# Loads of k and stores of the output with an outermost dimension of 32 or more rows, in a thresholded-attention and MoE kernel

## The chip, the cores and the metric

The kernel runs on one core of one Trainium2 chip. The metric is device microseconds of one execution. Each time below is the median of a kernel's runs, and every experiment ran beside the kernel before on the same chip (983.7, 983.4, 982.4, 985.3 and 989.2 us in the five sets), so sets can be compared through that.

Five engines work side by side: PE (matrix products; PEld in the views is its weight loads), DVE, ACT and POOL (elementwise work), and SP, which here only issues DMA transfers. Sixteen DMA engines carry out the transfers.

## The reference

```python
# q, k, v: (8 batches, 8 heads, 576 rows, 64), float32; w_in: 512 x 2048; w_out: 2048 x 512
scores = q @ k.T / 8
scores = where(scores >= max(scores) - 0.02, scores, -1e9)
attn = softmax(scores)
x = (attn @ v)                      # heads side by side: (4608, 512)
h = x @ w_in
out = maximum(0.01 * h, h) @ w_out  # (4608, 512), float32
```

## The kernel before

The work is cut into 160 steps, 20 to a batch of the inputs: five row chunks `c` times four head pairs `p`. A step computes scores on PE, finds the row maximum on DVE, takes the exponentials on ACT (`E` for one head; for the other a scaled copy `P`, whose exponential goes into `w` a step later), masks on DVE, divides by the sum on POOL (`w`), turns `w` around with a transposing DMA (`wt`), and multiplies by v on PE five steps later (`LAG`). MoE products are spread between the steps. Meanwhile each batch prepares k and q of the next one: load, cast to two float16 halves on ACT and POOL (`ks`, `qs`, two buffers each), transpose by DMA (`kst`, `qst`).

The parts that the change and the argument touch:

```python
    def load_qk(b, hb):
        ...
        src_q = q[b, ds(4 * hb, 4), :, :].rearrange("(g h) (p t) d -> h p g (t d)", h=2, t=9)
        src_k = k[b, ds(4 * hb, 4), :, :].rearrange("(g h) (x p t) d -> x h p g (t d)", h=2, x=2, t=9)
        for g in range(2):
            for x in range(2):
                nc.sync.dma_start(out=km[ds(64 * x, 64), g, :], in_=src_k[x, :, :, g, :])
            if b == 0:
                nc.sync.dma_start(out=qm[:, g, :], in_=src_q[:, :, g, :])
        ...
    def rows_of(b, c):
        if c == 4:
            return out[ds(b * S, 2 * S), :].rearrange("(b p t) d -> t b p d", t=9, b=2)[8]
        return out[ds(b * S, S), :].rearrange("(p t) d -> t p d", t=9)[ds(2 * c, 2)]
    # ... cut: the steps; a finished group of 128 rows is stored with
    nc.sync.dma_start(out=G.stores[m], in_=osb)
    # ... cut: the main loop, at the end of each step
        if evac:
            evac()
        for t in tick.get(s, []):   # loads, casts and transposes that prepare the next batch
            t()
```

A k load takes 32 rows of each of two heads, which don't join into one run of rows, so its outermost dimension is the two heads. A store takes two rows (2c and 2c+1) of each of 64 groups of nine, written with those two outermost: 2 x 64 x 512.

The order in which instructions stand on each engine is not the order of this text: a scheduler sets it when the program is built, and the engines then keep to it.

Of the kernel before, what the change touches and what calls it, by code (L numbers as in the profile page):

```python
# [12 lines left out]
AF = mybir.ActivationFunctionType  # L13
# [3 lines left out]
def kernel(  # L17
# [16 lines left out]
    nc = tc.nc  # L34
    B, H, S, D = q.shape
# [39 lines left out]
    def load_qk(b, hb):  # L75


        qm = sb.tile([128, 2, 576], FP32, tag="qm", bufs=2, name="qm")
        km = sb.tile([128, 2, 576], FP32, tag="km", bufs=2, name="km")
        src_q = q[b, ds(4 * hb, 4), :, :].rearrange("(g h) (p t) d -> h p g (t d)", h=2, t=9)  # L80
        src_k = k[b, ds(4 * hb, 4), :, :].rearrange("(g h) (x p t) d -> x h p g (t d)", h=2, x=2, t=9)
        for g in range(2):
            for x in range(2):
                nc.sync.dma_start(out=km[ds(64 * x, 64), g, :], in_=src_k[x, :, :, g, :])
            if b == 0:
                nc.sync.dma_start(out=qm[:, g, :], in_=src_q[:, :, g, :])
        if b > 0:
            nc.sync.dma_start(out=qm[:, :, :], in_=src_q)
        qms[b, hb], kms[b, hb] = qm, km

    def load_v(b):
# [106 lines left out]
    def h_unit(G, u):  # L198
        n = G.n
        per = 512 // n  # L200

        def mms():
            if u == 0:
                G.g = sb.tile([128, NJ, 256], FP16, tag="gT", bufs=2, name="gT")[:, :, 0:n]
            hp = ps.tile([128, per, n], FP32, tag="h", bufs=2, name="hp")
            for jj in range(per):
                j = u * per + jj
                for g in range(4):
                    nc.tensor.matmul(  # L209
                        out=hp[:, jj, :], lhsT=w_in16[:, g, ts(j, 128)], rhs=G.x[:, g, :],  # L210
                        start=(g == 0), stop=(g == 3), skip_group_check=True,
                    )

            def act():
                nc.scalar.activation(out=G.g[:, ds(u * per, per), :], in_=hp, func=AF.Relu, bias=0.0, scale=0.99)  # L215
                if (u + 1) * per == NJ:
                    for m in range(n // 128):
                        for c in range(4):
                            oq.append(lambda m=m, c=c: o_unit(G, m, c))
            return act  # L220
        return mms
# [47 lines left out]
    def rows_of(b, c):  # L269

        if c == 4:
            return out[ds(b * S, 2 * S), :].rearrange("(b p t) d -> t b p d", t=9, b=2)[8]
        return out[ds(b * S, S), :].rearrange("(p t) d -> t p d", t=9)[ds(2 * c, 2)]


    steps = []
# [9 lines left out]
    def group_of(b, c):  # L286

        if c == 4:
            key = ("t", b // 4)
            if key not in groups:  # L290
                t = b // 4
                groups[key] = Group(256, [rows_of(4 * t + 2 * m, 4) for m in range(2)])
            return groups[key], 64 * (b % 4), b % 4 == 3
        if b == B - 1 and c >= 2:
            if (b, c) not in groups:
                groups[b, c] = Group(128, [rows_of(b, c)])
            return groups[b, c], 0, True
        key = (b, c // 2, 0)
        if key not in groups:
            groups[key] = Group(256, [rows_of(b, 2 * (c // 2) + cc) for cc in range(2)])  # L300
        return groups[key], 128 * (c % 2), c % 2 == 1
# [41 lines left out]
    def pv(s):  # L343
        b, c, p = steps[s]
        wt = st[s]["wt"]
        vt = vts[b]
        n = 128 if c < 4 else 64
        if p == 0:
            pvt[0] = ps.tile([128, NP, n], FP32, tag="pv", bufs=1, name="pv")
        pvp = pvt[0]  # L350
        for j in range(5):
            for h in range(2):
                rhs = wt[:, 5 * h + j, :] if c < 4 else wt[:, j, ds(64 * h, 64)]
                nc.tensor.matmul(  # L354
                    out=pvp[ds(64 * h, 64), p, :], lhsT=vt[:, 2 * p + h, j, :], rhs=rhs,
                    start=(j == 0), stop=(j == 4), skip_group_check=True,
                    tile_position=(0, 64 * h),
                )
        if p == NP - 1:
            G, col, done = group_of(b, c)  # L360

            def evac():
                nc.scalar.activation(out=G.x[:, :, ds(col, n)], in_=pvp, func=AF.Copy, bias=0.0, scale=1.0)
                if done:
                    for u in range(NJ * G.n // 512):
                        hq.append(h_unit(G, u))
            return evac
        return None
# [30 lines left out]


    load_qk(0, 0)
    load_qk(0, 1)
    prep_q = deque()
    for p in range(NP):
# [9 lines left out]
    for g in range(4):  # L414
        nc.gpsimd.dma_start(
            out=w_out16[:, ds(4 * g, 4), :],
            in_=moe_w_out[ds(512 * g, 512), :].rearrange("(j p) d -> p j d", p=128))

    tick = {}
    for b in range(1, B):  # L420
        s0 = 20 * (b - 1)
        tick.setdefault(max(0, s0 - 4), []).append(lambda b=b: load_qk(b, 0))
        tick.setdefault(s0 + 12, []).append(lambda b=b: load_v(b))
        tick.setdefault(s0 + 4, []).append(lambda b=b: load_qk(b, 1))
        for p in range(NP):
            for i, t in enumerate(prep_tasks(b, p)):
                tick.setdefault(s0 + 1 + 4 * p + (i * 4) // 7, []).append(t)
# [7 lines left out]
    for s in range(NS + LAG + 1):  # L435
# [15 lines left out]
        if live:  # L451
            d = st[s]
# [19 lines left out]
        if live:  # L472
            nc.vector.scalar_tensor_tensor(  # L473
                out=d["W"][:, 0, 0:576], in0=s32, scalar=tb[:, 0:1], in1=E,
# [22 lines left out]
    while hq or oq:  # L497
        for q_ in (hq, oq):
            if q_:
                f = q_.popleft()()  # L500
# [37 lines left out]
```

## Time and profile before

| | before |
|---|---|
| time | 983.67 us (981.94 to 985.41) |
| PE, DVE, ACT, POOL busy | 61%, 54%, 46%, 45% |
| mean granted clock of PE | 0.857 |
| DMA engines, hardware queue | 87.6% of their time in packets |
| bytes moved | 115.8 MB, 118 GB/s |

Lines of the page of the kernel before. PEclk, DMA and GB/s have one value for each of 40 slices of the span, in tenths of full for the first two; q1 is the hardware DMA queue with packets, MB and share of 16 engines' span.

```profile
span 981.9 us, 14544 instructions
...
PE 600.4 (61%) x4880; PEld 373.7 (38%) x4880; DVE 528.8 (54%) x1580; ACT 453.2 (46%) x894; POOL 439.7 (45%) x572
...
PEclk9999977787858876878679997878799899989999
DMA  3999989999979699999999999998897998849720
...
q1 hardware_dynamic: 324768, 105.94, 87.6%
```

No compute engine is near full, but the DMA row is at 9 almost everywhere. In this count a DMA engine is busy while a packet is under way, also while that packet waits (18 packets that stand still for over 4 us are shown below).

The list of waits of the kernel before: who waited for what, us in total, how often, the longest.

```profile
ACT qs L155 <- DMA qst<-qs: 143.5, 25, 15.0
PE pv L354 <- DMA wt<-w: 117.1, 30, 11.2
...
PE sc L326 <- DMA qst<-qs: 107.6, 5, 55.7
```

PE and ACT wait for transposes. One place shows why. This is the timeline of the kernel before between 417 and 431 us; columns are start, duration, engine, line, operation, and in brackets the idle time just before and what ended it. A span on SPq is the time that SP took to issue.

```profile
417.08 0.58 SPq L241 DMA_DIRECT2D out_dram<-osb  x1
...
418.77 11.96 SPq L397 DMA_TRANSPOSE wt<-w  x4
...
421.33 0.47 PE L354 MATMUL pv<-wt,v 128*64 128x128 f16 x10 [0.52 <-ACT xT L363]
...
429.05 0.74 PE L354 MATMUL pv<-wt,v 128*64 128x128 f16 x10 [7.24 <-DMA wt<-w]
```

A store is issued at 417.08. The transposes behind it take long to issue, and PE stands idle for 7.24 us because a transpose hasn't landed. The packets that started in each microsecond of that stretch, counted from the trace's packet records (2,048 B are the store's, 256 B the transposes'; the k and q loads' left out):

```
us      store packets   transpose packets
420          11               278
421          24               192
422          26                 0
423          24                 0
424          26                 0
425          17                36
426           0              1015
```

While the store drains, at about 25 packets a microsecond of 84 ns each, so with two packets in flight, no transpose packet starts for three microseconds; when it ends, over a thousand start in one. The transposes are not merely queued: 18 of their packets, started by 421.9 us, stay in flight until 426.05 to 426.10 us, just after the store's last packet ended at 425.87. Over the whole span, two-engine copies (0.5 to 5 packets of a k load or store in flight, averaged over 0.1 us) are in flight for 427 us, and in 370 us of that fewer than 10 transposes' packets start in 0.1 us, against 73 otherwise when they flow. Wider copies (more than 5 packets in flight) run for 40 us.

### The profile page before, as it was taken

Reading aid. Unit: us, or ns where it says so; the run is one execution under the profiler, and the core shown is the slowest. Engines: PE = TensorE matmul, PEld = TensorE weight load, DVE = VectorE, ACT = ScalarE, POOL = GpSimd, SP = SyncE. Lnnn points to the kernel's source line nnn. Section 1 sums busy time; section 2 is a strip of 40 time slices with the busy share of each in tenths; the row PEclk is TensorE's granted clock in tenths of the full one; section 3 lists DMA queues with packets and bytes.
Section 4 is the critical chain, followed back from the end, with each engine's and each line's share of the span. In section 5 each row is a group of like instructions: output and inputs, shape, how many; then the busy total and the mean of one; then the engine's idle time right before and its main releaser. Section 6 shows DMA issues by size and latency. Waiting matters only on the chain. (4 is left out here: it accounts for less than half of the span.)

```text
span 981.9 us, 14544 instructions
## 1 busy us (share of the span) xinstructions
PE 600.4 (61%) x4880; PEld 373.7 (38%) x4880; DVE 528.8 (54%) x1580; ACT 453.2 (46%) x894; POOL 439.7 (45%) x572
## 2 busy tenths in 40 slices
PE   0010457555547534764549874775599669799995
PEld 0000133333324322542335542443366445565662
DVE  0040276564756614645438763654578568777800
ACT  2020255463644523544436563544567556665820
POOL 4250276273645533335535563624665654443500
PEclk9999977787858876878679997878799899989999
DMA  3999989999979699999999999998897998849720
GB/s 83 101 140 83 134 160 176 120 139 127 146 91 143 99 116 97 129 137 125 126 102 135 120 139 98 120 132 116 131 166 98 143 142 107 109 85 107 104 59 33
DMA packets 348651, 115.78 MB, mean 118 GB/s; under 512 B 333216, under 2 KB 335264, under 8 KB 348576
## 3 DMA queue, kind: packets, MB, share of 16 engines
q1 hardware_dynamic: 324768, 105.94, 87.6%
q0 software_dynamic: 23808, 8.92, 10.9%
q8 instruction: 38, 0.62, 0.3%
q14 instruction: 37, 0.30, 0.2%
HBM read 36.70 MB, written 9.44 MB: 47 GB/s over the span
## 5 line engine op out<-in xcount | busy, mean ns | idle before, releaser
L392 POOL TENSOR_SCALAR w<-w,rc 128x576 f16<-128x576 f16 x288 | 248.3, 873 | 284.0 <-DVE rc L390 268.1
L326 PE MATMUL sc<-kst,qst 128*128 128x288 f16 x1024 | 193.3, 319 | 190.0 <-DMA qst<-qs 107.6
L377 DVE TENSOR_SCALAR_CACHE_REDUCE s<-sc 128x576 f32<-128x576 f32 x288 | 213.6, 747 | 176.2 <-PE sc L326 166.5
L326 PEld LDWEIGHTS <-qst 128*128 128x128 f16 x1024 | 102.1, 106 | 261.9 <-DMA qst<-qs 112.2
L473 DVE SCALAR_TENSOR_TENSOR w<-s,tb,E 128x576 f16<-128x576 f32 x160 | 149.3, 934 | 67.2 <-ACT E L459 57.7
L354 PE MATMUL pv<-wt,v 128*64 128x128 f16 (+1 forms) x1600 | 77.9, 238 | 160.6 <-DMA wt<-w 117.1
L209 PE MATMUL hp<-xT,win 128*128 128x256 f16 (+1 forms) x1216 | 171.3, 289 | 2.8 <-ACT gT L215 2.8
L231 PE MATMUL op<-wout,gT 128*128 128x512 f16 x576 | 162.6, 403 | 0.0
L459 ACT ACTIVATE E<-s,tb 128x576 f16<-128x576 f32 x160 | 122.1, 769 | 72.8 <-DVE tb L380 52.4
L354 PEld LDWEIGHTS <-v 128*64 128x64 f16 x1600 | 60.0, 122 | 198.4 <-issue 164.0
L209 PEld LDWEIGHTS <-win 128*128 128x128 f16 x1216 | 119.3, 105 | 33.6 <-issue 6.3
L471 ACT ACTIVATE P<-s,tb 128x576 f16<-128x576 f32 x128 | 98.1, 767 | 44.6 <-DVE tb L380 35.8
L215 ACT ACTIVATE gT<-hp 128x512 f16<-128x512 f32 x144 | 83.3, 583 | 63.7 <-PE hp L209 54.3
L492 ACT ACTIVATE w<-P 128x576 f16<-128x576 f16 x128 | 86.7, 677 | 49.4 <-DVE P L491 28.8
L380 DVE SCALAR_TENSOR_TENSOR tb<-cm,mx,ca 128x2 f32<-128x2 f32 x288 | 98.2, 347 | 1.0
L155 ACT ACTIVATE qs<-qm 128x576 f16<-128x576 f32 x32 | 21.8, 682 | 150.6 <-DMA qst<-qs 143.5
L231 PEld LDWEIGHTS <-gT 128*128 128x128 f16 x576 | 59.3, 103 | 76.1 <-issue 28.5
L112 ACT ACTIVATE ks<-km 128x256 f16<-128x256 f32 x64 | 23.8, 406 | 108.4 <-DMA kst<-ks 49.5
L226 PE MATMUL op<-wio,xT 128*128 128x512 f16 x144 | 59.1, 411 | 14.8 <-DVE osb L240 14.7
L163 POOL TENSOR_SCALAR qm<-qm 128x576 f32<-128x576 f32 x32 | 22.4, 701 | 101.4 <-ACT qs L155 96.8
L171 DVE COPY qs<-qs 128x576 f16<-128x576 f16 x32 | 15.9, 498 | 89.0 <-ACT qs L155 89.0
L127 POOL TENSOR_SCALAR km<-km 128x576 f32<-128x576 f32 x32 | 22.2, 693 | 82.6 <-ACT ks L118 70.9
(35 smaller groups left out, 446.4 us busy)
## 6 DMA issues: line engine op xcount, KB each, us to landing
km<-in_k_dram SPq DMA_DIRECT2D x64, 144.0 KB
out_dram<-osb SPq DMA_DIRECT2D x36, 256.0 KB
qm<-in_q_dram SPq DMA_DIRECT2D x14, 576.0 KB
v<-in_v_dram POOLq DMA_DIRECT2D x32, 128.0 KB, 7.9
wt<-w SPq DMA_TRANSPOSE x160
win<-in_moe_w_in_dram POOLq DMA_DIRECT2D x4, 512.0 KB, 23.1
wout<-in_moe_w_out_dram POOLq DMA_DIRECT2D x4, 512.0 KB, 32.8
qm<-in_q_dram SPq DMA_DIRECT2D x4, 288.0 KB
```

What stands on the lines that cost most here:

```text
L209: nc.tensor.matmul(out=hp[:, jj, :], lhsT=w_in16[:, g, ts(j, 128)], rhs=G.x[:, g, :], start=(g == 0), stop=(g == 3), skip_group_check=True,)
L215: nc.scalar.activation(out=G.g[:, ds(u * per, per), :], in_=hp, func=AF.Relu, bias=0.0, scale=0.99)
L231: nc.tensor.matmul(out=G.op, lhsT=G.g[:, j, ds(128 * m, 128)], rhs=w_out16[:, j, :], start=False, stop=(j == NJ - 1), skip_group_check=True,)
L326: nc.tensor.matmul(out=sc[:, half, 0:288], lhsT=qa[sk], rhs=ka[half], start=(sk == 0), stop=(sk == 1), skip_group_check=True,)
L354: nc.tensor.matmul(out=pvp[ds(64 * h, 64), p, :], lhsT=vt[:, 2 * p + h, j, :], rhs=rhs, start=(j == 0), stop=(j == 4), skip_group_check=Tr ...
L377: nc.vector.tensor_scalar(out=halves(s32), in0=sc[:, :, 0:288], scalar1=C, scalar2=None, op0=AX.mult, op1=AX.max, accum_out=mx)
L380: nc.vector.scalar_tensor_tensor(out=tb, in0=cm[:, ds(2 * kind, 2)], scalar=mx, in1=ca[:, ds(2 * kind, 2)], op0=AX.mult, op1=AX.add)
L392: nc.gpsimd.tensor_scalar(out=W[:, h, 0:576], in0=W[:, h, 0:576], scalar1=rc[:, h : h + 1], scalar2=1.0, op0=AX.mult, op1=AX.mult,)
L459: nc.scalar.activation(out=E, in_=s32, func=AF.Exp, bias=tb[:, 1:2], scale=1.0)
L471: nc.scalar.activation(out=P, in_=s32b, func=AF.Identity, bias=tb2[:, 1:2], scale=KD)
L473: nc.vector.scalar_tensor_tensor(out=d["W"][:, 0, 0:576], in0=s32, scalar=tb[:, 0:1], in1=E, op0=AX.is_ge, op1=AX.mult, accum_out=d["sm"][ ...
L492: nc.scalar.activation(out=d["W"][:, 1, 0:576], in_=P, func=AF.Exp, bias=0.0, scale=1.0 / KD, accum_out=d["sm"][:, 1:2],)
```

## The change

The intent is that k loads and stores use all 16 DMA engines. The Trainium skill ("DMA: Bandwidth & Descriptors", section "Why a DMA increments its semaphore by 16 and not by 1") says that a transfer runs on the largest number of engines up to 16 that divides the slowest non-size-1 dimension of both its sides. So the k loads are cut by head into transfers of 32 partitions, and a store's rows are written with the 64 row groups outermost. The second needs the columns of `xT` interleaved, which the copy out of PSUM now does with a stride.

```diff
-        for g in range(2):
+        gs = [ds(0, 1), ds(1, 1)] if b == 0 else [ds(0, 2)]
+        for g in gs:
             for x in range(2):
-                nc.sync.dma_start(out=km[ds(64 * x, 64), g, :], in_=src_k[x, :, :, g, :])
-            if b == 0:
-                nc.sync.dma_start(out=qm[:, g, :], in_=src_q[:, :, g, :])
-        if b > 0:
-            nc.sync.dma_start(out=qm[:, :, :], in_=src_q)
+                for h in range(2):
+                    nc.sync.dma_start(out=km[ds(64 * x + 32 * h, 32), g, :], in_=src_k[x, h, :, g, :])
+            nc.sync.dma_start(out=qm[:, g, :], in_=src_q[:, :, g, :])
@@ rows_of
-            return out[...].rearrange("(b p t) d -> t b p d", t=9, b=2)[8]
-        return out[...].rearrange("(p t) d -> t p d", t=9)[ds(2 * c, 2)]
+            return out[...].rearrange("(b p t) d -> t p b d", t=9, b=2)[8]
+        return out[...].rearrange("(p t) d -> p t d", t=9)[:, ds(2 * c, 2), :]
@@ evac
-                nc.scalar.activation(out=G.x[:, :, ds(col, n)], in_=pvp, func=AF.Copy, bias=0.0, scale=1.0)
+                if c < 4:
+                    xo = G.x[:, :, ds(col, 128)].rearrange("f g (p i) -> f g i p", i=2)
+                    xi = pvp.rearrange("f g (i p) -> f g i p", i=2)
+                else:
+                    m, i = divmod(col // 64, 2)
+                    xo = G.x[:, :, ds(128 * m, 128)].rearrange("f g (p i) -> f g i p", i=2)[:, :, i, :]
+                    xi = pvp
+                nc.scalar.activation(out=xo, in_=xi, func=AF.Copy, bias=0.0, scale=1.0)
```

More of the change, by code (lines that the diff above doesn't have):

```diff
@@ L271, in rows_of @@
         if c == 4:
-            return out[ds(b * S, 2 * S), :].rearrange("(b p t) d -> t b p d", t=9, b=2)[8]
-        return out[ds(b * S, S), :].rearrange("(p t) d -> t p d", t=9)[ds(2 * c, 2)]
+            return out[ds(b * S, 2 * S), :].rearrange("(b p t) d -> t p b d", t=9, b=2)[8]
+        return out[ds(b * S, S), :].rearrange("(p t) d -> p t d", t=9)[:, ds(2 * c, 2), :]
     steps = []
```

## The prediction

> **What bounds the kernel now.** The engine totals name no bound (page: PE 61%, DVE 54%, ACT 46%, POOL 45% of 981.9 us), but the DMA row stands at 9 in nearly every slice while 118 GB/s move: the DMA engines mostly wait.
>
> The packet records say why. A store of a 2x64x512 output tile (128 packets of 2,048 B) takes 5.1 to 7.1 us with 2.0 packets in flight; a k load (64 packets of 2,304 B) also runs at 2.0. The q loads and the four tail-group stores, whose outermost dimension is 128, run with 12 to 16 in flight; such a store takes about 1 us. So k loads and 32 of 36 stores use two DMA engines, as the Trainium skill states ("DMA: Bandwidth & Descriptors", "Why a DMA increments its semaphore by 16 and not by 1"): the engine count is the largest number up to 16 that divides the outermost non-1 dimension of both sides. This trace agrees.
>
> The cost is what stands behind the copy. Transposes (303,104 packets of 256 B) go through the same SP queue on all engines. Two-engine copies are in flight for 427 us; in 370 us of that, transposes nearly stop. 1,730 transpose packets took over 0.5 us each and hold 335 of the transposes' 766 us per engine; the median packet takes 18 ns. SP's issue spans show backpressure: a wt transpose takes 1.2 us at least, 2.05 at the median; SP spends 813 us issuing. In the list of waits PE is behind wt 117 us, behind qst 108.
>
> **What changes.** k loads become transfers of 32 partitions, outermost 32: 16 engines. Stores become 64 rows outermost: 16 engines, about 1 us each. Two-engine time goes from 427 us to almost nothing, 16-engine time from 40 to about 90. Added: eight DMA issues (0.55 us each) and a strided ACT write of xT (32 of them, 583 ns now, perhaps 0.1 us more): negligible.
>
> **How much is on the critical path.** Not all 370 us. In the last batch (863 to 928 us) steps take 3.43 us although stores still starve transposes, because there PE is 96% busy at clock 0.97. The other batches (now 83 to 144 us per 20 steps) fall towards that. DVE's 529 us are 3.3 us per step, nearly the same floor.
>
> Sum of estimates:
> - start until step 2: 109 us now, some 35 of it transposes behind two-engine k loads: about 75
> - 158 steps at about 3.75 us (floor 3.43, more where k and q preparation run beside): 592, now 819
> - tail after the last step: 53 now, its last two stores 11.4: about 44
>
> Total about 712 us; range 670 to 770. Faster by over 2%: 0.97; same: 0.02; slower: 0.01.
>
> **What would show it.** Store bursts near 1 us with over 10 packets in flight; wt issue median 1.3 to 1.5 us, SP's issue total near 430 us; q1's share of the engines falling from 88% to about 50%; PE's waits behind wt and qst down by two thirds; PE busy above 78%, granted clock above 0.9; 20 steps in about 75 us.
>
> **What would make it wrong.** If transposes are limited by something else, packets stay long and the gain is under 150 us. If PE, DVE, POOL and transposes, all near 3.3 to 3.7 us per step, disturb one another, steps stay near 4.2 us and the time lands above 770.

## The result, and the profile after

The changed kernel takes 793.49 us (793.01 to 793.97), against 983.67: a ratio of 0.807, interval 0.800 to 0.813. Here and below a ratio is the record's ratio of fast runs, which is not quite the ratio of the medians. The gain is 190 us where 272 were forecast, and the time lies above the forecast's range.

The same lines of the page of the changed kernel:

```profile
span 791.2 us, 14565 instructions
...
PE 579.1 (73%) x4880; PEld 363.8 (46%) x4880; DVE 532.0 (67%) x1580; ACT 455.5 (58%) x894; POOL 441.2 (56%) x572
...
PEclk9999598999999899898898789989999899899999
DMA  9999999999969998998699976899499946354501
...
q1 hardware_dynamic: 326240, 105.95, 74.9%
```

The list of waits of the changed kernel:

```profile
PE sc L325 <- DVE s L384: 66.9, 56, 5.6
...
PE sc L325 <- DMA qst<-qs: 62.3, 7, 20.9
...
ACT qs L154 <- DMA qst<-qs: 54.8, 16, 18.7
...
PE pv L353 <- DMA wt<-w: 30.0, 20, 6.1
```

And the timeline of the changed kernel around one of its stores:

```profile
410.47 1.25 SPq L240 DMA_DIRECT2D out_dram<-osb  x1
411.78 1.39 SPq L176 DMA_TRANSPOSE qst<-qs  x1
413.27 2.20 SPq L404 DMA_TRANSPOSE wt<-w  x1
413.42 0.74 PE L353 MATMUL pv<-wt,v 128*64 128x128 f16 x10 [3.77 <-DMA wt<-w]
...
415.56 1.30 SPq L144 DMA_TRANSPOSE kst<-ks  x1
416.97 1.26 SPq L404 DMA_TRANSPOSE wt<-w  x1
```

The transposes behind this store are issued in 1.3 to 2.2 us each. PE still waits 3.77 us here, for a transpose that must have been issued before the store, since the next of `wt` is issued only from 413.27 on. From the packet records: a store lasts 0.91 us at the median (0.69 to 2.57) where the two-engine ones lasted about 6.4 us, usually with 12 to 15 packets in flight; two-engine copies are in flight for 29 us instead of 427 (some of that is the starts and ends of the wide copies, which the measure counts too). Wide copies run for 108 us (forecast about 90), and in 98 us of that transposes nearly stop: the copies stop the transposes in either form, and the change shortened the stop, from 406 us (370 + 36) to 115 (17 + 98). The median wt issue fell from 2.05 to 1.36 us. PE waits 30 us for `wt` instead of 117. So the two-engine copies went, and with them most of the stop. What it gave is best read in three terms, from the times of the exponentials `E`, one in each step:

| us | before | forecast | changed |
|---|---|---|---|
| start until the third step's exponential | 114 | 75 | 53 |
| steps from there to the last | 814 | 592 | 690 |
| from the last step's exponential to the end | 54 | 44 | 48 |

(The forecast counted the start to PE's first product of that step, 109 us before.) The start gained more than forecast. The steps gained less by 98 us, more than the whole error of 81 us, of which start and tail take back about 18. Part of this split is where the line is drawn: in the changed kernel a gap of 19 us follows the third exponential, where the kernel before has 5 us. Counted to the fourth exponential the start went from 119 us to 72, against about 80 forecast there, and the steps missed by 82 us.

The change also shows what it costs: the strided copy of `xT` on ACT takes 729 ns instead of 583 (32 of them; 448 instead of 373 for the 8 small ones), 5 us over the span.

### The profile page after: what moved, and what is told of

It reads as the page before. It is cut to its first block, busy times and chain, and to the rows that moved or that the text cites. A ratio compares the mean times of both kernels' runs of the same rounds, so it can differ in the third digit from the quotient of the medians.

```text
span 791.2 us, 14565 instructions
## 1 busy us (share of the span) xinstructions
PE 579.1 (73%) x4880; PEld 363.8 (46%) x4880; DVE 532.0 (67%) x1580; ACT 455.5 (58%) x894; POOL 441.2 (56%) x572
## 3 DMA queue, kind: packets, MB, share of 16 engines
q1 hardware_dynamic: 326240, 105.95, 74.9%
## 5 line engine op out<-in xcount | busy, mean ns | idle before, releaser
L325 PE MATMUL sc<-kst,qst 128*128 128x288 f16 x1024 | 188.0, 312 | 129.5 <-DVE s L384 66.9
L325 PEld LDWEIGHTS <-qst 128*128 128x128 f16 x1024 | 98.8, 104 | 197.7 <-issue 85.8
L466 ACT ACTIVATE E<-s,tb 128x576 f16<-128x576 f32 x160 | 122.1, 768 | 96.5 <-DVE tb L387 85.4
L208 PE MATMUL hp<-xT,win 128*128 128x256 f16 (+1 forms) x1216 | 164.9, 283 | 3.0 <-ACT gT L214 3.0
L230 PE MATMUL op<-wout,gT 128*128 128x512 f16 x576 | 157.8, 395 | 0.0
L353 PE MATMUL pv<-wt,v 128*64 128x128 f16 (+1 forms) x1600 | 73.3, 229 | 61.9 <-ACT xT L370 31.6
L499 ACT ACTIVATE w<-P 128x576 f16<-128x576 f16 x128 | 86.6, 677 | 43.3 <-DVE P L498 26.9
L387 DVE SCALAR_TENSOR_TENSOR tb<-cm,mx,ca 128x2 f32<-128x2 f32 x288 | 103.0, 364 | 1.1
L353 PEld LDWEIGHTS <-v 128*64 128x64 f16 x1600 | 56.7, 117 | 100.2 <-issue 93.8
L154 ACT ACTIVATE qs<-qm 128x576 f16<-128x576 f32 x32 | 21.8, 680 | 57.0 <-DMA qst<-qs 54.8
L498 DVE TENSOR_SCALAR P<-P 128x576 int16<-128x576 int16 x128 | 48.6, 380 | 6.8 <-ACT P L478 6.5
L170 DVE COPY qs<-qs 128x576 f16<-128x576 f16 x32 | 12.8, 399 | 57.2 <-ACT qs L154 57.2
L239 DVE COPY osb<-op 128x512 f32<-128x512 f32 x36 | 24.5, 681 | 38.1 <-PE op L230 38.1
```

Source lines behind the costliest of these rows:

```text
L208: nc.tensor.matmul(out=hp[:, jj, :], lhsT=w_in16[:, g, ts(j, 128)], rhs=G.x[:, g, :], start=(g == 0), stop=(g == 3), skip_group_check=True,)
L230: nc.tensor.matmul(out=G.op, lhsT=G.g[:, j, ds(128 * m, 128)], rhs=w_out16[:, j, :], start=False, stop=(j == NJ - 1), skip_group_check=True,)
L325: nc.tensor.matmul(out=sc[:, half, 0:288], lhsT=qa[sk], rhs=ka[half], start=(sk == 0), stop=(sk == 1), skip_group_check=True,)
L353: nc.tensor.matmul(out=pvp[ds(64 * h, 64), p, :], lhsT=vt[:, 2 * p + h, j, :], rhs=rhs, start=(j == 0), stop=(j == 4), skip_group_check=Tr ...
L387: nc.vector.scalar_tensor_tensor(out=tb, in0=cm[:, ds(2 * kind, 2)], scalar=mx, in1=ca[:, ds(2 * kind, 2)], op0=AX.mult, op1=AX.add)
L466: nc.scalar.activation(out=E, in_=s32, func=AF.Exp, bias=tb[:, 1:2], scale=1.0)
```

## The experiments

Two questions were tried: whether the gain came from the engine count, and where the forecast's 98 us in the steps went. Names in the edits are those of the code above.

### Each half alone

`e1_k_only` takes the change's k loads only, `e2_store_only` the stores and the `xT` copy only.

```diff
 e1: before, with the new load_qk;  rows_of and evac as before
 e2: before, with the new rows_of and evac;  load_qk as before
```

> Only the k loads changed, stores as before. Theory (engine count; each two-engine copy stops the transposes behind it, about 213 us of k loads and 200 us of stores): the start shortens as in the full change (second-step start near 53 us instead of 114) and the steps gain about half of what they gained in the full change (814 to 690 us): about 860 us in all (ratio 0.87). Rival (the halves hide behind each other, so that one alone gives little until the other is gone): 920 us or more.

> Only stores and the xT write changed, k loads as before. Theory: the start stays at 114 us, the steps gain about half, the tail a few us: about 915 us (ratio 0.93), and the gains of this run and of k loads alone add up to about the 190 us of the full change. Rival (halves hide behind each other): under 30 us of gain in this one.

Measured: k alone 841.65 us (ratio 0.856, 0.853 to 0.859), stores alone 928.49 us (0.945, 0.941 to 0.949). The halves gain 142 and 55 us, in sum 197, where both together gain 190: they add up, so the rival falls. The start is the k loads' part: third exponential at 52 us with k alone, at 110 with stores alone. Two-engine copies were in flight for 218 us in the first and 243 us in the second. The split was expected near 123 and 68, so k was worth more than half and the stores less.

### Outermost 62 instead of 64

The change is named after "32 or more rows". This run keeps the changed kernel but cuts each store into 62 and 2 rows, so that the outermost dimension is far over 32 but shares only 2 with a power of two (62 = 2 x 31, 124 partitions = 4 x 31).

```diff
-                nc.sync.dma_start(out=G.stores[m], in_=osb)
+                nc.sync.dma_start(out=G.stores[m][0:62], in_=osb[0:124])
+                nc.sync.dma_start(out=G.stores[m][62:64], in_=osb[124:128])
```

> The changed kernel with each store cut into one of 62 rows and one of 2. If the number of DMA engines is the largest number up to 16 that divides the outermost dimensions (62 and 124: 2), each large store takes about 6 us with 2 packets in flight again, and the time rises to about 840, as with k loads alone changed. If 32 or more outermost rows are enough, a store takes about 1 us and the time rises by less than 15 us, for the added issues.

Measured: 830.27 us (0.843, 0.841 to 0.846). The stores take 6.40 us at the median with 2.0 packets in flight, against 0.91 us, also the four of the tail group that were wide before. This agrees with the skill's rule: what counts is what divides the dimension, not its size. It also puts a cost on two-engine stores by adding it: 37 us for 36 stores over the changed kernel, with the cost of 36 added issues in it. That is somewhat less than the 48 us by which k alone is slower than the full change, and 10 us less than was expected here.

### More buffers for the casts

Over the span of the changed kernel, ACT waited 55 us at `qs` and 18 us at `ks` for transposes that still read the buffer (35 and 12 us of it between 75 us and the last step). First attempt, `e3_bufs3`: three buffers instead of two.

```diff
-            ks = sb.tile([128, 9, 128], FP16, tag="ks", bufs=2, name="ks")
+            ks = sb.tile([128, 9, 128], FP16, tag="ks", bufs=3, name="ks")
-            qs = sb.tile([128, 2, 9, 128], FP16, tag="qs", bufs=2, name="qs")
+            qs = sb.tile([128, 2, 9, 128], FP16, tag="qs", bufs=3, name="qs")
```

> The changed kernel with three instead of two buffers for qs and ks. Theory A of the missing 80 us (ACT stands in order behind a qs or ks buffer that a queued transpose still reads; 55 us behind qst and 18 behind kst in the list of waits): these waits fall to under 20 us and the time falls by 25 to 60 us, to about 735 to 765. Rival B (PE, DVE and the rest disturb each other at their shared floor, whatever the buffers): the time stays within 1% of 793.

Measured: 790.86 us (0.805, 0.802 to 0.807), the same as the changed kernel. ACT still waits 36 us at `qs` for transposes and more for the loads (21 us at `ks`). So theory A as stated fell: a third buffer doesn't do it. The trace shows a possible reason that this run can't separate: with a buffer free, the scheduler moved some casts of q still further ahead, two of them by 11 and 13 steps (422 of the 894 places of ACT's order hold another instruction). Four buffers were not run: the build doesn't fit (it needs 212.4 kb where 207.9 are left).

### What preparation costs

`e4_noprep` leaves out all preparation of batches 1 to 7 (they read batch 0's k and q, so the result is wrong). `e5_noturn` leaves out the k and q transposes of those batches and keeps loads and casts; `e6_turnonly` keeps the transposes, of batch 0's tiles, and leaves out loads and casts.

```diff
 e4
-        tick ... load_qk(b, 0), load_qk(b, 1), all of prep_tasks(b, p)
-        qst, kst = qsts[b, p], ksts[b, p]
+        qst, kst = qsts[0, p], ksts[0, p]
 e5
             for i, t in enumerate(prep_tasks(b, p)):
+                if i in (2, 6):      # kturn, qturn
+                    continue
-        qst, kst = qsts[b, p], ksts[b, p]
+        qst, kst = qsts[0, p], ksts[0, p]
 e6
-        tick ... load_qk(b, 0), load_qk(b, 1)
             for i, t in enumerate(prep_tasks(b, p)):
+                if i in (2, 6):      # they read the ks and qs tiles that batch 0 left
                     tick...append(t)
```

> Wrong on purpose: the k and q loads, casts and transposes of batches 1 to 7 are left out, every batch reads those of batch 0. Theory A (preparation costs the steps their pace): every batch takes 65 to 72 us per 20 steps, as the last one does in the changed kernel, and the time is about 660 to 680. Rival B (the engines disturb each other also without preparation): batches stay above 78 us and the time above 720.

> Wrong on purpose: as the run without preparation, but only the k and q transposes of batches 1 to 7 are left out; loads and casts stay. Theory D (the preparation's transposes, a third of all transpose packets, slow the others): about 680 to 700, most of the 125 us comes back. Theory E (the casts on ACT, POOL and DVE and their place in the engines' order cost it): 750 or more.

> Wrong on purpose: the k and q transposes of batches 1 to 7 stay, but read the tiles of batch 0, so the loads and the casts are left out. Theory D: 750 or more. Theory E: about 680 to 700. If both this and the run without transposes lie near the middle, the two causes add up; if both are near 680, only their coupling (a cast that waits for a transpose) costs the time.

Measured: 666.74 us without preparation (0.681, 0.678 to 0.683), 727.3 without its transposes (0.741, 0.737 to 0.744), 747.31 with its transposes alone (0.761, 0.757 to 0.765). Without preparation batches 1 to 6 take 64 to 73 us for 20 steps (one 80), against 77 to 101 in the changed kernel. Stretches of the changed kernel and of the one without preparation, from the third step's exponential to the last one's, one line each (stretch, its length, busy us and instructions of PE, PEld, DVE, ACT and POOL, granted clock, DMA share, GB/s):

```profile
53.00:743.00 690.00, 531.77 (x4510) 336.61 (x4511) 512.15 (x1529) 428.81 (x840) 404.67 (x512) 0.91 0.89 152
```

```profile
62.00:613.00 551.00, 487.47 (x4511) 319.68 (x4511) 458.16 (x1475) 381.74 (x701) 264.09 (x312) 0.98 0.68 110
```

Without preparation PE is busy for 88% of the stretch, 487 of 551 us, and DVE for 83%; with it, PE for 77% and DVE for 74%. So preparation costs 127 us of the changed kernel's 793. Its own instructions keep DVE busy for 54 us more, ACT for 47 and POOL for 141, but none of them is full. Leaving out either half gives back 66 or 46 us, 112 of the 127 in sum: neither theory's "most of it" held. Each of these builds has its own instruction order, so the split is rough.

### The casts kept in their step

Where do preparation and steps collide? This is ACT in the changed kernel, with three lines of DVE from the same timeline (438 to 449 us):

```profile
437.73 0.71 ACT L111 ACTIVATE ks<-km 128x256 f16<-128x256 f32 x2
438.34 0.51 ACT L117 ACTIVATE ks<-km 64x64 f16<-64x64 f32 x2
...
439.17 0.30 DVE L498 TENSOR_SCALAR P<-P 128x576 int16<-128x576 int16 x1
...
439.39 0.21 DVE L387 SCALAR_TENSOR_TENSOR tb<-cm,mx,ca 128x2 f32<-128x2 f32 x1
...
447.27 0.68 ACT L154 ACTIVATE qs<-qm 128x576 f16<-128x576 f32 x1 [8.43 <-DMA qst<-qs]
...
447.86 0.67 ACT L499 ACTIVATE w<-P 128x576 f16<-128x576 f16 x1
447.99 0.33 DVE L170 COPY qs<-qs 128x576 f16<-128x576 f16 x1 [7.71 <-ACT qs L154]
...
448.43 0.19 ACT L499 ACTIVATION_READ_ACCUMULATOR w<-P 128x1 f32 x1
448.52 0.76 ACT L466 ACTIVATE E<-s,tb 128x576 f16<-128x576 f32 x1
```

A cast of q for the next batch (L154) stands in front of two exponentials (L499, L466), and waits 8.43 us for a transpose to release its buffer. The inputs of both were ready on DVE at 439.47 and 439.60 us (L498, L387), but the exponentials behind the cast don't pass it: the skill ("TensorE: Matmul & The Clock Gate", part 1, under the queue depths) says that ACT and DVE are strict FIFO, and this trace agrees: they start at 447.86 and 448.52, and DVE stands 7.71 us in front of its own copy of the same `qs` (L170). Such bunches recur: at one place of the changed kernel's ACT order, nine casts (`ks` five times, `qs`, `ks` twice, `qs`) and two copies to `xT` stand between one exponential and the next.

`e7_inorder_act` puts an order edge, without a wait, from the step's `E` on ACT to the casts that are written after it, so that the scheduler can't move them ahead of it. `e8_inorder_all` does so on DVE, POOL and SP too. The edit of the first, shortened:

```diff
-            nc.scalar.activation(out=E, in_=s32, func=AF.Exp, bias=tb[:, 1:2], scale=1.0)
+            last_act = nc.scalar.activation(out=E, in_=s32, func=AF.Exp, bias=tb[:, 1:2], scale=1.0)
 ...
-        for t in tick.get(s, []):
-            t()
+        with ExitStack() as after:
+            if tick.get(s):
+                after.enter_context(tc.issue_after(last_act.ins))
+            for t in tick.get(s, []):
+                t()
```

> The changed kernel with the casts of k and q held on ACT behind the exponential of the step they are written in (an order edge, no wait), so that the scheduler no longer bunches them ahead of a step's work. Theory C (ACT stands, in its fixed order, before casts that were moved up and whose loads or buffers are late): ACT's waits at the casts fall from about 95 us to under 30 and the time falls to about 730 to 760. Rival (the cost is the amount of work, not its place): within 1% of 793.

> The same with the order held on ACT, DVE, POOL and SP. Theory C: at least as good as on ACT alone, 720 to 760. Rival: within 1% of 793, or slower since SP and POOL lose freedom.

Measured: 746.05 us with ACT held (0.758, 0.754 to 0.761) and 748.02 with all held (0.761, 0.758 to 0.764), both correct. That is 47 us under the changed kernel with no work removed. The waits of ACT at its casts, between 75 us and the last step; first all such lines of the changed kernel:

```profile
ACT qs L154 <- DMA qst<-qs: 35.4, 14, 8.4
...
ACT ks L111 <- DMA km<-in_k_dram: 12.3, 2, 8.9
ACT ks L111 <- DMA kst<-ks: 12.0, 7, 2.8
...
ACT ks L117 <- DMA km<-in_k_dram: 3.8, 2, 3.5
ACT ks L111 <- issue: 3.2, 2, 2.6
...
ACT ks L117 <- issue: 0.6, 1, 0.6
ACT qs L154 <- DMA qm<-in_q_dram: 0.5, 1, 0.5
```

and then with ACT's casts in order, where one line is left:

```profile
ACT ks L117 <- DMA km<-in_k_dram: 0.4, 1, 0.4
```

So 68 us of waiting in ACT's fixed order became 0.4, and 47 us of time came back. Theory C held. Holding the other engines added nothing. The stretch from the third step's exponential to the last one's, in the run with ACT held, shows the same work in 646 us instead of 690:

```profile
50.00:696.00 646.00, 517.75 (x4509) 331.19 (x4510) 511.37 (x1527) 429.42 (x839) 399.96 (x512) 0.93 0.96 162
```

### The same order in the kernel before

```diff
 before, with the edge of e7 on ACT; nothing else
```

> The kernel before, with the casts of k and q held in order on ACT as in the run that did so to the changed kernel. If the two-engine copies are what limits the kernel before, whatever its order, the time stays within 2% of 983. If the order costs the same there, it falls by about 45 us to 938.

Measured: 972.27 us (0.988, 0.983 to 0.993), same at 2%. In the kernel before, ACT waited for 173 us at its casts between 115 us and the last step; with the edge for none. Yet the time fell by 12 us only, because the wait moved. The list of waits of this run:

```profile
PE pv L354 <- DMA wt<-w: 216.5, 54, 14.6
PE sc L326 <- DMA qst<-qs: 106.3, 6, 55.0
```

PE waits 217 us for `wt`, instead of 117. As long as two-engine copies stop the transposes for 370 us (372 in this run), it hardly matters in which order ACT works. Once they are gone, the same order costs 47 us.

### Order and buffers

```diff
 e7, with three buffers of ks and qs as in e3
```

> Casts in order on ACT and three buffers of qs and ks. With the order held the buffers are no longer waited for, so within 1% of 746.

Measured: 745.12 us (0.756, 0.753 to 0.759), as expected the same as with the order alone. With the casts in their step, two buffers are enough.

### Is the rest transposes or casts?

With the order held, preparation still costs 746 - 667 = 79 us. This run holds the order and leaves out the transposes.

```diff
 e7, with the edit of e5
```

> Wrong on purpose: casts in order on ACT and the k and q transposes of batches 1 to 7 left out. Without preparation the kernel took 667 us, with casts alone in the scheduler's order 727, with transposes alone 747, with both in held order 746. Theory F (once the casts are in order they hide, and the preparation's transposes carry what is left): 665 to 690. Rival G (the casts' work itself keeps its cost on ACT, POOL and DVE): 715 to 730.

Measured: 727.42 us (0.735, 0.731 to 0.738). Theory F fell, and G's time came out: loads and casts alone keep 60 us over the kernel without preparation, in order or not (727.3 in the scheduler's order). The transposes add 19 us once the order is held, where they added 66 before. (This set ran on another chip, where the kernel before took 989.2 us; by the ratios to it, 60 and 19 become 53 and 23.) Batches 2 to 6 take 84, 81, 82, 76 and 79 us without these transposes and 84, 85, 82, 76 and 81 with them: in the middle of the run the transposes are hidden. But so are the casts and loads behind the transposes. With the transposes alone (`e6_turnonly`, 747.31 us, where no casts are left to hold) the time is that of both in order (746.05), and its batches 2 to 6 take 80, 87, 82, 82 and 79 us. Once the order is held, then, leaving out casts and loads gives back nothing, leaving out the transposes 19 us, and leaving out both 79. Each of the two alone costs 60 us or more and hides most of the other, so neither can be called the cause of the 79. The 46 us that came back when casts and loads were left out of the changed kernel are just what holding their order gives back (47 us).

Casts and loads can be told apart in one place. In batch 6 of the run without transposes (`e13_inorder_noturn`; batches counted from 0) no packet of a k or q load runs, only the casts for batch 7, and it takes 79 us where the kernel without preparation takes 69. In `e5_noturn` the casts and loads all fall into batches 0 to 3, and its batches 4 to 6 take 70, 69 and 69 us, like those without preparation. So in batch 6 the casts cost the 10 us without any load beside them; this is one stretch of one execution.

### The weights loaded later

The changed kernel and the one with casts in order both show a gap of 19 to 20 us between the third and the fourth step's exponential, while the two weight matrices (8 MB) load and the first batch's transposes stand beside them. This run starts from `e7` and moves those loads to steps 1 to 4.

```diff
+    for g in range(4):
+        tick.setdefault(1 + g // 2, []).append(lambda g=g: load_w(g))
+        tick.setdefault(3 + g // 2, []).append(lambda g=g: load_wo(g))
-        the same loads among the first 28 preparation tasks
-                after.enter_context(tc.issue_after(last_act.ins))
+                after.enter_context(...)      # in steps 0 to 5 also behind POOL's last w
```

> The changed kernel with casts in order on ACT, and the loads of the two weight matrices moved from among the first preparations to steps 1 to 4. Theory: the gap of 20 us before the fourth step (transposes of the first batch behind the weight loads) goes, the first batch takes 80 to 90 us instead of 103, and the time falls from 746 to about 730. Rival: the weights are then waited for later, and the time stays at 746.

Measured: 730.97 us (0.743, 0.740 to 0.747), correct, 62 us under the changed kernel. The mechanism was only half as expected. The first exponential comes at 27 us instead of 37, but the gap of 20 us only splits into 9 and 12 us and the first batch still takes 103 us from there; it is the second batch that falls, from 82 to 73.

## Why the prediction was wrong

It named the mechanism rightly, as far as the runs show it, and sized one term wrongly. Point by point:

- **Two-engine copies stop the transposes: right.** Stores went from about 6.4 us to 0.91, two-engine time from 427 to 29 us, wt issues from 2.05 to 1.36 us, each forecast. The halves add up (142 and 55 us), and bringing the two engines back by a row count of 62 costs 37 us again.
- **Start, forecast 75 us, measured 53: a miss in the kernel's favour,** but a small one when counted to the fourth exponential (72 us against about 80), since a gap of 19 us falls just after the third. It is the k loads' part: with k alone the third comes at 52 us.
- **Tail, forecast 44 us, measured 48.** Nearly right.
- **"158 steps at about 3.75 us (floor 3.43, more where k and q preparation run beside): 592": this step failed.** They took 690 us, 4.39 each over the 157 intervals. The floor itself was right: the last batch, which prepares nothing, takes 65 us in both kernels, and without preparation all steps take 551 us, 3.5 each. What was mis-sized is the allowance for preparation: 0.32 us a step, about 50 us. It measured 690 - 551 = 139 us in the steps, 127 in whole times. (About 10 of the 139 are early gaps that fall before the third exponential without preparation, at 62 us, and after it in the changed kernel, at 53; counted from the first exponential it is 129.) Of the 139,
  - 44 us (690 - 646; 47 in whole times) are the place of the casts in ACT's order. Kept in their step, they cost that much less. The kernel before had this wait too, 144 us of `qs` behind `qst` in its list of waits, and the prediction doesn't name it. With the two-engine copies gone it fell to 55 us but did not vanish. In the kernel before the cure was worth 12 us: there its cost was hidden behind the copies;
  - 95 us (646 - 551; 79 in whole times) are what preparation costs in order. It can't be put on one half: with loads and casts alone 60 us stay, with transposes alone 81 (747 - 667), with both 79. Which engine's work it is that sets the pace there was not tried: in that stretch PE is at 80%, DVE at 79%, ACT at 66% and POOL at 62%.
- **q1's share of the DMA engines "about 50%", SP issuing "near 430 us": wrong.** They were 74.9% and 550 us. Of PE's waits, "down by two thirds", the one behind `wt` was (117 to 30 us), the one behind `qst` not (108 to 62). Transpose packets still take 25.9 ns on average at a median of 18. What holds them then was not tried.
- **PE above 78%, clock above 0.9: half right,** 73% and 0.92. The skill ("TensorE: Matmul & The Clock Gate", part 1) says the PE clock is throttled by default and activity releases it. The traces agree: their clock records hold 0.5 and 1.0 only, and the mean over the span goes 0.857, 0.92, 0.941, 0.987 from the kernel before through the changed one and the one in order to the one without preparation, as PE's gaps shrink.
- **The other warning was near:** "If PE, DVE, POOL and transposes [...] disturb one another, steps stay near 4.2 us and the time lands above 770". The outcome was that one, at 4.39. About a third of the cost of preparation (47 of 127 us) was an instruction order that can be changed; whether the other 79 us are such a shared limit was not tried, but that each half hides the other would fit it.

Open: why the transposes stop on the other 14 DMA engines while two engines drain a copy. The records show that packets of a transpose stand in flight meanwhile and end together with the copy; the records name no engine, so what holds them is not shown. That transposes are issued behind it on the same queue, and SP's issue spans stretch, fits, but no run put the copies on another queue. Open too is which engine's work makes each half of preparation cost what it does.

## What to carry to other kernels

Count the packets in flight during a copy: two, where its neighbours have twelve or more, meant here that the outermost dimension divides badly, and the cost was everything queued behind the copy, not its bytes. Before adding up what such a repair gives, measure the kernel's pace in a stretch that has no side work, and measure the side work as a term of its own, by a run that leaves it out; here it was put at 50 us and cost 127. Leave out each part alone as well as all of them: of two parts that hide each other, each looks cheap. After a DMA repair look again at waits inside an in-order engine: an early cast that waits holds up all that stands behind it, and here an order edge, which removes no work, gave a quarter as much as the repair itself.

## What the Trainium skill lacked or had wrong

- "DMA: Bandwidth & Descriptors", "Rules for kernel authors", row "Use all 16 engines": it tells that an outermost dimension below 16 confines a transfer to few engines, and the section on the semaphore has the rule of the divisor, which held (outermost 2 and 62: 2.0 packets in flight; 64 and 128: mostly 12 to 15 over a store; 32: 15 to 19 at the peak of a k load). It gives no measured time of a transfer on few engines. Here a 256 KB store took about 6.4 us on two engines and 0.91 us on sixteen.
- The same page says that such a copy uses few engines, but not that transposes issued behind a copy on the same queue nearly stop meanwhile: in 370 of 427 us of two-engine copies and 36 of 40 us of wider ones. Shortening copies of about 18 MB, of the 116 that move, took 190 us off 984.
- The same page has no time measured on trn2 for issuing a transpose from SP. Here one of `wt` (128 x 5 x 128 or 128 x 10 x 128 elements) took 1.2 us at least, 1.36 at the median in the changed kernel, and up to 10.0 in the kernel before.
- "TensorE: Matmul & The Clock Gate" states that ACT is strict FIFO. None of the pages read says what that costs where a scheduler moves side work ahead: 68 us of waits on ACT and 47 us of time here.
